# The opening of a fused convolution and gated-MLP kernel: first columns of w_in by another queue, two taps to TensorE, scaling and loads in another order

## The chip, the cores and the metric

The kernel runs on one core of a Trainium2 chip. The metric is device time in microseconds (us) of a whole execution. The engines are TensorE (PE; its weight loads are shown as PEld), VectorE (DVE), ScalarE (ACT), GpSimd (POOL) and SyncE (SP). Each executes its own instructions in order. DMAs are issued by SP, ACT or POOL, each in a queue of its own, and carried by 16 DMA engines that the queues share. A DMA that changes the type (fp32 to bf16) is issued by POOL here; the others by SP or ACT.

## The reference

The input x has 8 batches of 4096 tokens with 192 channels. A causal convolution of 7 taps runs over the tokens, its weights being a softmax over the taps for each of 8 heads of 24 channels. The result goes through a gated layer without a gate matrix of its own:

```python
w = np.exp(weight - np.max(weight, axis=-1, keepdims=True))
w = w / (np.sum(w, axis=-1, keepdims=True) + 1e-09)          # (8 heads, 7 taps)
out = np.einsum('hk,bskhg->bshg', w, x_unf)                  # x_unf: 7 shifted copies of x
h = out.reshape(32768, 192) @ w_in                           # w_in (192, 2048)
g = h * (1.0 / (1.0 + np.exp(-beta * h)))                    # beta (2048,)
y = g @ w_out                                                # w_out (2048, 192)
```

The kernel computes silu(beta * h) and multiplies w_out by 1/beta, which gives the same. x, w_in, w_out and beta are fp32 in memory; the large matrix products are done in bf16.

## The kernel before, in words

**Stages and units.** The tokens are cut into 32 chunks; a chunk is 512 tokens of two batches at once. Channels lie on partitions: a group is 64 channels (rows 0 to 63 for one batch, 64 to 127 for the other), and there are NG = 3 groups. One chunk is one stage `s`, and a stage has 16 units `u`, one for each block of 128 columns of w_in. `hidden` (L409) does six matmuls of a unit into a PSUM tile ph, and one ScalarE activation (L417) writes g from it. `output` (L442) does matmuls of g with w_out in pairs, into two PSUM tiles pa and pb, spread over the units behind. From stage 1 on a unit has 8 pairs; in stage 0 units 3 and 7 have 5 pairs into pa alone and units 8 to 15 have 5 each; what is left over is done after the last stage. Finished sums go through VectorE (L460) and an SP DMA.

**Convolution.** For chunks from 2 on, x is cast, transposed by DMA and convolved on VectorE tap by tap (`tap`, L331 and L333), a stage ahead, out of a `queue` of seven taps. In stage 0 the order of such work is written out by hand in `first_work`: for each unit a list, in which `None` takes the next tap from the queue.

**The opening.** Chunks 0 and 1 are done differently, and all of this stands ahead of the units or in stage 0:
- SP issues x of chunk 0 (x0, two DMAs), x of chunk 1 (x1, two), the first two quarters of w_out (w_out_raw), x of chunk 2 (xf, two), the other two quarters, x of chunk 3. ACT issues weight and beta.
- POOL builds a selection matrix `sel` and an identity, then issues w_in, as bf16, into w_in_s: columns 0 to 255 for each half of the partitions (two DMAs, L208), then, after a tiny copy `hold` that waits for the first cast of x0, columns 256 to 511 and the three other quarters of 512 columns, two DMAs each.
- The softmax: VectorE takes the maximum on 8 partitions, ScalarE the exponentials and their sum, and a matmul with `sel` spreads them to 128 partitions (L254), where VectorE divides, which gives cw. beta is transposed by TensorE (L258) and copied by ScalarE (L259).
- `fill` (L226) gives TensorE matmuls of zeros where it would be idle.
- x0 is cast (VectorE, L231), transposed by TensorE (L238) and copied to xt0 by ScalarE (L299). VectorE builds `diag`, seven diagonal matrices of cw (L302). Groups 0 and 1 of chunk 0 are convolved by TensorE, seven matmuls with `diag` each (L284), and copied out to ct by ScalarE (L326); group 2 is convolved by VectorE in seven taps, which end in ct too. In between ScalarE casts x1 to x1b (L231), two blocks after each group's matmuls.
- VectorE scales the first quarter of w_out by 1/beta (`scale_w_out`, L311). The other three quarters are scaled by it from `first_work`.
- Unit 0 of stage 0 does the hidden matmuls of units 0 and 1 group by group, then `second` transposes x1b on TensorE (L353) and copies it out on VectorE (L362). Group 0 of chunk 1 is convolved by TensorE in units 4 to 6 (`CONV1`) and copied out by VectorE (`conv1_evac`, L388); its groups 1 and 2 are the seven taps of the queue. `rows_of(2)` casts chunk 2 and starts its transposes.

Of the kernel before, what the change touches and what calls it, by code (L numbers as in the profile page):

```python
# [9 lines left out]
FP32 = mybir.dt.float32  # L10
FP32R = mybir.dt.float32r
BF16 = mybir.dt.bfloat16
AF = mybir.ActivationFunctionType
ALU = mybir.AluOpType
# [3 lines left out]
def kernel(  # L18
# [17 lines left out]
    nc = tc.nc  # L36

    B, S, D = x.shape
    H, K = weight.shape
    F = moe_w_in.shape[1]  # L40
    group = D // H
    DG = 64
    NG = D // DG
    HP = group // NG
    TOK = 512
    NF = F // 128
    PAD = K - 1
    HALO = 16
# [7 lines left out]
    NB = TOK // BLK  # L56
# [4 lines left out]
    consts = ctx.enter_context(tc.tile_pool(name="consts", bufs=1))  # L61
    setup = ctx.enter_context(tc.tile_pool(name="setup", bufs=1))
# [18 lines left out]
    def in_a():  # L81
        return psum_a.tile([128, 2, TOK], FP32, name="pa")
# [50 lines left out]
    NW = 4  # L133
    FW = F // NW
# [11 lines left out]
    def load_w_out(i):  # L146
        fcs = slice(i * NQ, (i + 1) * NQ)
        nc.sync.dma_start(out=w_out_raw[:, fcs, :], in_=w_out_v[:, fcs, :])

    e8 = setup.tile([H, K + 1], FP32)  # L150
    cw8 = setup.tile([H, K], FP32)
    beta_q = setup.tile([NF, 128], FP32)
    nc.scalar.dma_start(out=cw8, in_=weight)
    nc.scalar.dma_start(out=beta_q, in_=moe_beta.rearrange("(c p) -> c p", p=128))


    def load_x(dst, t0):
        for i in range(2):
            t = t0 + i * 2 * BLK
            nc.sync.dma_start(  # L160
                out=dst[:, i].rearrange("q h b d -> q h (b d)"),
                in_=x_v[0, t : t + 2 * BLK, :, :].rearrange(
                    "(q b) h d -> q h (b d)", b=2
                ),
            )

    load_x(x0, 0)
    load_x(x1, TOK)
    load_w_out(0)
    load_w_out(1)  # L170
    load(2)
    load_w_out(2)
    load_w_out(3)
    load(3)

    zeros = setup.tile([128, TOK], BF16)
    nc.vector.memset(zeros, 0.0)
    warm = setup.tile([H, 1], FP32)
    nc.vector.memset(warm, 0.0)  # L179
    nc.scalar.activation(warm, warm, AF.Exp)  # L180

    sel = setup.tile([H, 2, DG], FP32)
    nc.gpsimd.memset(sel, 1.0)
# [22 lines left out]
    def load_w_in(c0, c1):  # L206
        for r in range(2):
            nc.gpsimd.dma_start(  # L208
                out=w_in_s[r * DG : (r + 1) * DG, :, c0:c1], in_=w_in_v[:, :, c0:c1]
            )  # L210

    load_w_in(0, FW // 2)

    nmax = setup.tile([H, 1], FP32)
    nc.vector.reduce_max(nmax, cw8, axis=mybir.AxisListType.X, negate=True)
    nc.scalar.activation(
        e8[:, 0:K], cw8, AF.Exp, bias=nmax, accum_out=e8[:, K : K + 1]
    )
    nc.scalar.activation(warm, warm, AF.Silu)
    ident_b = setup.tile([128, 128], BF16)  # L220
    nc.vector.tensor_copy(ident_b, ident)
    pf = psum_h.tile([128, 2, TOK], FP32, name="ph")

    def fill(n, cols=TOK):
        for _ in range(n):
            nc.tensor.matmul(  # L226
                pf[:, 0, 0:cols], zeros[:, 0:128], zeros[:, 0:cols], start=True, stop=True
            )

    def cast_rows(copy, xb, x, b):  # L230
        copy(  # L231
            xb[:, b].rearrange("q c h p -> q h c p"),
            x[:, b // 2, :, b % 2].rearrange("q h (p c) -> q h c p", c=NG),
        )
# [7 lines left out]
    def tokens(xt, b):  # L242
        t = HALO + (b // 2) * 2 * BLK
        return xt[:, :, t : t + 2 * BLK].rearrange("p c (q b) -> p c b q", b=2)[:, :, b % 2]

    beta = consts.tile([128, NF], FP32)
    beta_r = setup.tile([128, NF], FP32)
    cw = consts.tile([128, K], FP32)
    rn = setup.tile([128, 1], FP32)

    fill(5)
    pc = in_a()
    pw, pb = pc[:, 0, 0 : K + 1], pc[:, 1, 0:NF]
    nc.tensor.matmul(  # L254
        pw, sel.rearrange("i h p -> i (h p)"), e8, start=True, stop=True
    )
    fill(1, 256)
    nc.tensor.transpose(pb, beta_q, ident[0:NF, 0:NF])  # L258
    nc.scalar.copy(beta, pb)  # L259
    for b in range(2):  # L260
        cast_rows(nc.vector.tensor_copy, x0b, x0, b)
    nc.vector.reciprocal(rn, pw[:, K : K + 1])
    nc.vector.tensor_scalar_mul(cw, pw[:, 0:K], rn)
    for b in range(2, NB):
        cast_rows(nc.vector.tensor_copy, x0b, x0, b)

    hold = setup.tile([1, 1], BF16)
    nc.gpsimd.tensor_copy(hold, x0b[0:1, 0, 0, 0, 0:1])  # L268
    load_w_in(FW // 2, FW)
    for i in range(1, NW):  # L270
        load_w_in(i * FW, (i + 1) * FW)

    diag = setup.tile([128, K, 128], FP32R)
    xt0 = setup.tile([128, NG, HALO + TOK], FP32R)
    nc.vector.memset(xt0[:, :, 0:HALO].bitcast(FP32), 0.0)
    xt1 = setup.tile([128, HALO + TOK], FP32R)
    cts = {}

    def new_ct(s):
        cts[s] = ct_pool.tile([128, NG, TOK], BF16, name="ct")  # L280

    def diag_tap(k, xt, pv, rows=slice(0, 128)):
        o = HALO - PAD + k
        nc.tensor.matmul(  # L284
            pv,
            diag[rows, k, :],
            xt[rows, o : o + TOK],
            start=(k == 0),
            stop=(k == K - 1),
        )  # L290

# [4 lines left out]
    for b in range(NB):  # L296
        pt = pts[b % 2][:, b // 2, 0 : NG * BLK].rearrange("p (c q) -> p c q", c=NG)
        transposes(pt, x0b, b)
        nc.scalar.copy(tokens(xt0, b), pt)  # L299
        fill(1, 256 if b % 2 else 128)  # L300
    fill(1, 256)
    nc.vector.tensor_tensor(  # L302
        diag,
        ident.unsqueeze(1).to_broadcast((128, K, 128)),
        cw.unsqueeze(2).to_broadcast((128, K, 128)),
        ALU.mult,
    )

    def scale_w_out(i):
        fcs = slice(i * NQ, (i + 1) * NQ)  # L310
        nc.vector.tensor_tensor(  # L311
            w_out_s[:, fcs, :],
            w_out_raw[:, fcs, :],
            beta_r[:, fcs].unsqueeze(2).to_broadcast((128, NQ, D)),
            ALU.mult,
        )
# [3 lines left out]
    for c in range(NG - 1):  # L320
        pv = in_b() if c else psum_h.tile([128, 2, TOK], FP32, name="ph")
        for k in range(K):
            diag_tap(k, xt0[:, c], pv[:, 0, :])
        for b in range(2):
            cast_rows(nc.scalar.copy, x1b, x1, 2 * c + b)
        nc.scalar.copy(cts[0][:, c, :], pv[:, 0, :])  # L326

    def tap(dst, src, k):
        scalar = cw[:, k : k + 1]
        if k == 0:  # L330
            nc.vector.tensor_scalar_mul(dst, src, scalar)  # L331
        else:
            nc.vector.scalar_tensor_tensor(  # L333
                out=dst, in0=src, scalar=scalar, in1=dst, op0=ALU.mult, op1=ALU.add
            )

    for k in range(K):
        o = HALO - PAD + k
        tap(cts[0][:, NG - 1, :], xt0[:, NG - 1, o : o + TOK].bitcast(FP32), k)
    nc.vector.reciprocal(beta_r, beta)  # L340
    scale_w_out(0)

# [164 lines left out]
    def rows_of(ch):  # L507
        for h in range(2):
            cast(ch, h)
        xpose(ch)  # L510


    first_work = {
        4: [None],
        5: [lambda: scale_w_out(1), None],
        7: [None, conv1_evac],
        8: [None],
        9: [lambda: scale_w_out(2)],
        10: [None, lambda: rows_of(2)],
        11: [None],  # L520
        12: [lambda: scale_w_out(3), None],
    }

    queue = deque()
    for s in range(N_ST):
        jobs_of(s)
        for u in range(NF):
            if s > 0 or u > 1:
                hidden(s, u)
            elif u == 0:  # L530
                phs = [hidden(0, fc, [0]) for fc in range(2)]
                for j in range(1, NG):
                    for fc in range(2):
                        hidden(0, fc, [j], phs[fc])
                second()
            if s > 0:
                output(s, u, 8 if s < N_ST - 1 else 7, "ab")
            elif u > 7:
                output(s, u, 5, "ab")
            elif u == 3 or u == 7:  # L540
                output(s, u, 5, "a")
            if s == 0:
                if u in CONV1:
                    conv1(u)
                if u == min(CONV1):
                    queue.extend(conv_ops(1, 1))
                for work in first_work.get(u, []):
                    (work or queue.popleft())()
            else:
                if u % 2 and queue:  # L550
                    queue.popleft()()

                if u == 0 and s + 3 < N_CH:
                    load(s + 3)
                if u < 2 and s + 2 < N_CH:
                    cast(s + 2, u)
                if u == 1 and s + 2 < N_CH:
                    xpose(s + 2)
            if u == 12 and s + 2 < N_CH:
                queue.extend(conv_ops(s + 2, 0))  # L560
# [32 lines left out]
```

## Time and profile before

| what | value |
|---|---|
| median of 10 runs | 692.58 us (692.06 to 693.34) |
| profiled execution | 692.36 us |
| its span, first to last instruction | 690.6 us |
| busy: PE, ACT, DVE, POOL | 683.7, 579.1, 527.1, 8.1 us |
| chain that ended last | PE 96%, DMA 2%, DVE 1% |
| first g of stage 0 (L417) starts | 13.63 us |
| first hidden matmuls of stage 1 start | 31.43 us |

The times are counted from the span's start. The chain is followed back from the last instruction, at each step to what released it. In rows of the timeline the columns are start, duration, engine, line, operation, what is written and read with its shape, the count of merged instructions, and in brackets the idle time of the engine ahead of it with what ended it. Ends of matmuls are modelled. DMA queue q1 is SP's, q10 ACT's, q0 POOL's.

### The profile page before, as it was taken

To read this page: it belongs to the slowest core of one execution; us is meant where nothing else is said; L and a number is where in the kernel's file an instruction comes from. 1 tells how busy PE (TensorE), PEld (TensorE's weight loads), DVE (VectorE), ACT (ScalarE), POOL (GpSimd) and SP (SyncE) were. 2 spreads that over 40 slices of the span, in tenths; PEclk is the share of its full clock that TensorE was granted. 3 is DMA by queue.
4 is the path that set the end of the run, shared out by engine and by line. 5 is a ranking of instruction groups with operands and counts; after the bars stand their busy time and mean duration, and the time that the engine had idled before them with its cause. 6 is when DMAs were issued, how large, how long until landed. Compare 5 with 4: busy or idle time off the path is not lost.

```text
span 690.6 us, 24335 instructions
## 1 busy us (share of the span) xinstructions
PE 683.7 (99%) x11310; PEld 496.5 (72%) x11310; DVE 527.1 (76%) x466; ACT 579.1 (84%) x531; POOL 8.1 (1%) x20
## 2 busy tenths in 40 slices
PE   8999999999999999999999999999999999999997
PEld 4677777777777777777777777777777777777776
DVE  7888877797777797777887777887777977777712
ACT  7888888888888888888888888888888888888893
POOL 4000000000000000000000000000000000000000
PEclk9999999999999999999999999999999999999999
DMA  9754332344332343332344432443323433322111
GB/s 219 170 117 116 93 104 70 83 116 113 91 104 59 100 116 104 97 98 60 108 116 94 104 83 70 116 116 93 104 62 92 116 107 97 104 54 60 48 37 59
DMA packets 121862, 66.86 MB, mean 97 GB/s; under 512 B 53265, under 2 KB 121761, under 8 KB 121761
## 3 DMA queue, kind: packets, MB, share of 16 engines
q1 hardware_dynamic: 119632, 63.73, 35.0%
q0 software_dynamic: 2080, 1.57, 1.5%
q8 instruction: 88, 1.44, 0.9%
q14 instruction: 14, 0.11, 0.1%
q10 hardware_dynamic: 48, 0.01, 0.0%
HBM read 29.89 MB, written 25.17 MB: 80 GB/s over the span
## 4 chain that ended last, share of the span: by engine, by line
PE 96%; DMA 2%; DVE 1%; POOL 0%; ACT 0%; issue 0%
PE ph L409 47%; PE pa L442 24%; PE pb L442 24%; DMA w_in_s<-in_moe_w_in_dram 2%; DVE ct L333 1%; DMA x<-in_x_dram 0%; PE pb L284 0%; POOL w_in_s L208 0%; DVE w_out_s L311 0%; DVE ct L388 0%; DVE xb L106 0%; ACT g L417 0%; DVE x0b L231 0%; ACT osb L458 0%; POOL hold L268 0%
## 5 line engine op out<-in xcount | busy, mean ns | idle before, releaser
L417 ACT ACTIVATE g<-ph,beta 128x1024 bf16<-128x1024 f32 x512 | 569.8, 1114 | 97.1 <-PE ph L409 91.2
L442 PEld LDWEIGHTS <-g 64*128 64x128 bf16 x8160 | 353.6, 94 | 120.9 <-ACT g L417 0.9
L409 PE MATMUL ph<-ct,w_in_s 64*128 64x512 bf16 x3072 | 417.0, 376 | 1.6 <-ACT g L417 0.7
L333 DVE SCALAR_TENSOR_TENSOR ct<-xt,cw,ct 128x1536 bf16<-128x1536 bf16 (+2 forms) x192 | 338.4, 1762 | 2.5
L442 PE MATMUL pa<-w_out_s,g 64*128 64x192 bf16 x4112 | 238.9, 243 | 0.6 <-ACT g L417 0.5
L442 PE MATMUL pb<-w_out_s,g 64*128 64x192 bf16 (+1 forms) x4048 | 224.9, 243 | 0.0
L409 PEld LDWEIGHTS <-w_in_s 64*128 64x128 bf16 x3072 | 142.8, 94 | 64.0 <-DMA w_in_s<-in_moe_w_in_dram 2.2
L460 DVE TENSOR_REDUCE osb<-pa 128x384 f32<-128x768 f32 x64 | 61.3, 958 | 121.5 <-PE pa L442 121.5
L460 DVE TENSOR_REDUCE osb<-pb 128x384 f32<-128x768 f32 x63 | 60.3, 958 | 28.9 <-PE pb L442 28.8
L106 DVE CAST xb<-xf 128x768 bf16<-128x768 f32 x60 | 40.7, 679 | 0.0
L331 DVE TENSOR_SCALAR ct<-xt,cw 128x1536 bf16<-128x1536 bf16 (+2 forms) x32 | 31.2, 974 | 0.2 <-ACT xt L299 0.2
L208 POOL DMA_DIRECT2D w_in_s<-in_moe_w_in_dram x10 | 6.5, 656 | 2.3 <-DMA w_in_s<-in_moe_w_in_dram 2.3
L458 ACT COPY osb<-pb 128x192 f32<-128x192 f32 x1 | 0.3, 319 | 6.7 <-PE pb L442 6.7
L226 PE MATMUL ph<-zeros 128*128 128x512 bf16 (+2 forms) x11 | 4.4, 493 | 1.3 <-DVE warm L179 1.3
L284 PE MATMUL pb<-xt,diag 64*128 64x512 f32 (+1 forms) x21 | 5.1, 445 | 0.0
L121 DVE COPY xt<-xt 128x18 bf16<-128x18 bf16 x27 | 4.3, 161 | 0.0
L311 DVE TENSOR_TENSOR w_out_s<-w_out_raw,beta_r 128x768 bf16<-128x768 f32 x4 | 3.8, 959 | 0.0
L284 PEld LDWEIGHTS pb<-xt,diag 64*128 64x128 f32 (+1 forms) x21 | 3.2, 187 | 0.8
L284 PE MATMUL ph<-xt,diag 128*128 128x512 f32 x7 | 2.8, 562 | 0.2 <-ACT xt L299 0.2
L226 PEld LDWEIGHTS <-zeros 128*128 128x128 bf16 x11 | 1.4, 139 | 2.1 <-DVE warm L179 1.3
L231 DVE CAST x0b<-x 128x384 bf16<-128x384 f32 x4 | 1.5, 408 | 1.8 <-DMA x<-in_x_dram 1.8
L180 ACT ACT_TABLE_LOAD x1 | 1.3, 1283 | 1.8 <-issue 1.8
(48 smaller groups left out, 25.0 us busy)
## 6 DMA issues: line engine op xcount, KB each, us to landing
out_dram<-osb SPq DMA_DIRECT2D x127, 192.0 KB, 2.1
xf<-in_x_dram SPq DMA_DIRECT2D x60, 384.0 KB, 4.2
xt<-xb SPq DMA_TRANSPOSE x120, 3.0
x<-in_x_dram SPq DMA_DIRECT2D x4, 384.0 KB, 4.5
w_out_raw<-in_moe_w_out_dram SPq DMA_DIRECT2D x4, 384.0 KB, 13.3
w_in_s<-in_moe_w_in_dram POOLq DMA_DIRECT2D x6, 192.0 KB, 11.7
w_in_s<-in_moe_w_in_dram POOLq DMA_DIRECT2D x4, 96.0 KB, 8.7
out_dram<-osb SPq DMA_DIRECT2D x2, 96.0 KB, 1.6
```

The lines of the kernel that those rows point to most:

```text
L106: nc.vector.tensor_copy(xbs[ch][:, :, :, h, :], xfs[ch][:, h].rearrange("q b (p c) -> q b c p", c=NG),)
L121: nc.vector.tensor_copy(dst, last[:, :, HALO + TOK - PAD :])
L208: nc.gpsimd.dma_start(out=w_in_s[r * DG : (r + 1) * DG, :, c0:c1], in_=w_in_v[:, :, c0:c1])
L226: nc.tensor.matmul(pf[:, 0, 0:cols], zeros[:, 0:128], zeros[:, 0:cols], start=True, stop=True)
L284: nc.tensor.matmul(pv, diag[rows, k, :], xt[rows, o : o + TOK], start=(k == 0), stop=(k == K - 1),)
L311: nc.vector.tensor_tensor(w_out_s[:, fcs, :], w_out_raw[:, fcs, :], beta_r[:, fcs].unsqueeze(2).to_broadcast((128, NQ, D)), ALU.mult,)
L331: nc.vector.tensor_scalar_mul(dst, src, scalar)
L333: nc.vector.scalar_tensor_tensor(out=dst, in0=src, scalar=scalar, in1=dst, op0=ALU.mult, op1=ALU.add)
L409: nc.tensor.matmul(ph[:, h, :], w_in_s[rows, j, fc * 128 : (fc + 1) * 128], cts[s][rows, j, :], start=(j == 0), stop=(j == NG - 1),)
L417: nc.scalar.activation(gs[s][:, fc], ph, AF.Silu, scale=beta[:, fc : fc + 1])
L442: nc.tensor.matmul(self.po[:, r, b * D : (b + 1) * D], g[rows, fc, self.h, q * BLK : (q + 1) * BLK], w_out_s[rows, fc, :], start=(self.don ...
L460: nc.vector.tensor_reduce(dst, self.po[:, :, 0 : nb * D].rearrange("p r n -> p n r"), axis=mybir.AxisListType.X, op=ALU.add,)
```

## The change

- **w_in.** Columns 0 to 255 are no longer loaded by POOL. SP loads them as fp32 into a new tile w_in_raw, for both halves of the partitions in one DMA whose source is broadcast over a leading dimension of 2, and ScalarE copies them to w_in_s as bf16. This copy stands after beta's copy and ahead of the casts of x1. POOL issues columns 256 to 511 and the three other quarters, all after `hold`: 8 DMAs instead of 10.
- **Loads on SP.** x0, then beta (from ACT's queue before), then w_in_raw, x1, three quarters of w_out, x of chunk 2, the last quarter, x of chunk 3.
- **Softmax.** The raw taps are spread to 128 partitions by the matmul first; maximum, exponentials, sum and division are then done there. `diag` is built in three pieces, the first between the casts of x0.
- **Group 2 of chunk 0.** Taps 5 and 6 are done by TensorE in two matmuls, taps 0 to 4 by VectorE, which then adds the two.
- **Scaling of w_out's first quarter** is done by GpSimd.
- **Order.** The tile of zeros has 128 columns and is broadcast; the fills have other numbers and places; xt0's halo is cleared earlier; beta's transpose comes after those of x0; the last cast of x1 stands after the copies to ct.
- **Stage 0.** `first_work` is rewritten: the scaling of quarters 1, 2 and 3 is in units 4, 6 and 8 (5, 9 and 12 before), conv1_evac and rows_of(2) in unit 6 (7 and 10), the seven taps in units 4, 4, 5, 6, 8, 9, 10 (4, 5, 7, 8, 10, 11, 12). Units 4 and 7 have 2 and 5 output pairs into pa, unit 15 has 10: 52 pairs in all instead of 50. `CONV1` is as before.

```diff
-    e8 = setup.tile([H, K + 1], FP32)
-    cw8 = setup.tile([H, K], FP32)
+    w8 = setup.tile([H, K], FP32)
+    nc.scalar.dma_start(out=w8, in_=weight)
     beta_q = setup.tile([NF, 128], FP32)
-    nc.scalar.dma_start(out=cw8, in_=weight)
-    nc.scalar.dma_start(out=beta_q, in_=moe_beta.rearrange("(c p) -> c p", p=128))
...
     load_x(x0, 0)
+    nc.sync.dma_start(out=beta_q, in_=moe_beta.rearrange("(c p) -> c p", p=128))
+    F0 = 256
+    w_in_raw = setup.tile([128, NG, F0], FP32)
+    nc.sync.dma_start(
+        out=w_in_raw, in_=w_in_v[:, :, 0:F0].unsqueeze(0).to_broadcast((2, DG, NG, F0))
+    )
     load_x(x1, TOK)
-    load_w_out(0)
-    load_w_out(1)
+    for i in range(NW - 1):
+        load_w_out(i)
     load(2)
-    load_w_out(2)
-    load_w_out(3)
+    load_w_out(NW - 1)
     load(3)
...
-    load_w_in(0, FW // 2)
-
-    nmax = setup.tile([H, 1], FP32)
-    nc.vector.reduce_max(nmax, cw8, axis=mybir.AxisListType.X, negate=True)
-    nc.scalar.activation(
-        e8[:, 0:K], cw8, AF.Exp, bias=nmax, accum_out=e8[:, K : K + 1]
-    )
...
+    fill(3)
+    pw = in_a()[:, 0, 0:K]
+    nc.tensor.matmul(pw, sel.rearrange("i h p -> i (h p)"), w8, start=True, stop=True)
+    fill(5)
...
+    nc.vector.reduce_max(nmax, pw, axis=mybir.AxisListType.X, negate=True)
+    nc.scalar.activation(cw, pw, AF.Exp, bias=nmax, accum_out=total)
+    nc.scalar.activation(warm, warm, AF.Silu)
+    nc.vector.reciprocal(total, total)
+    nc.vector.tensor_scalar_mul(cw, cw, total)
...
-    for b in range(2):
+    for b in range(NB):
         cast_rows(nc.vector.tensor_copy, x0b, x0, b)
...
+        if b == 1:
+            diags(0, 2)
+    diags(2, 4)
+    diags(4, K)
...
     nc.gpsimd.tensor_copy(hold, x0b[0:1, 0, 0, 0, 0:1])
-    load_w_in(FW // 2, FW)
+    load_w_in(F0, FW)
     for i in range(1, NW):
         load_w_in(i * FW, (i + 1) * FW)
...
         nc.scalar.copy(tokens(xt0, b), pt)
-        fill(1, 256 if b % 2 else 128)
+        if b % 2:
+            fill(1, 384)
+    pb = in_a()[:, 0, 0:NF]
+    nc.tensor.transpose(pb, beta_q, ident[0:NF, 0:NF])
+    nc.scalar.copy(beta, pb)
     fill(1, 256)
...
+    nc.scalar.copy(w_in_s[:, :, 0:F0], w_in_raw)
...
-        nc.vector.tensor_tensor(
+        (nc.vector if i else nc.gpsimd).tensor_tensor(
             w_out_s[:, fcs, :],
...
-        for b in range(2):
-            cast_rows(nc.scalar.copy, x1b, x1, 2 * c + b)
+        for b in ((0, 1), (2,))[c]:
+            cast_rows(nc.scalar.copy, x1b, x1, b)
         nc.scalar.copy(cts[0][:, c, :], pv[:, 0, :])
+    cast_rows(nc.scalar.copy, x1b, x1, NB - 1)
...
-    for k in range(K):
+    K_V = 5
+    pv = in_a()[:, 0, :]
+    for k in range(K_V, K):
+        diag_tap(k, xt0[:, NG - 1], pv, k0=K_V)
+    dst = cts[0][:, NG - 1, :]
+    for k in range(K_V):
         o = HALO - PAD + k
-        tap(cts[0][:, NG - 1, :], xt0[:, NG - 1, o : o + TOK].bitcast(FP32), k)
+        tap(dst, xt0[:, NG - 1, o : o + TOK].bitcast(FP32), k)
+    nc.vector.tensor_tensor(dst, pv, dst, ALU.add)
...
     first_work = {
-        4: [None],
-        5: [lambda: scale_w_out(1), None],
-        7: [None, conv1_evac],
-        8: [None],
-        9: [lambda: scale_w_out(2)],
-        10: [None, lambda: rows_of(2)],
-        11: [None],
-        12: [lambda: scale_w_out(3), None],
+        4: [None, lambda: scale_w_out(1), None],
+        5: [None],
+        6: [conv1_evac, lambda: scale_w_out(2), lambda: rows_of(2), None],
+        8: [None, lambda: scale_w_out(3)],
+        9: [None],
+        10: [None],
     }
 
+    QUOTA_A = {4: 2, 7: 5}
...
-                output(s, u, 5, "ab")
-            elif u == 3 or u == 7:
-                output(s, u, 5, "a")
+                output(s, u, 5 if u < NF - 1 else 10, "ab")
+            elif u in QUOTA_A:
+                output(s, u, QUOTA_A[u], "a")
```

`diags(k0, k1)` is a new function around the multiplication of L302, for the taps k0 to k1.

More of the change, by code (lines that the diff above doesn't have):

```diff
@@ L167 @@
     load_x(x0, 0)
+    nc.sync.dma_start(out=beta_q, in_=moe_beta.rearrange("(c p) -> c p", p=128))
[4 more added lines that the diff above has]
+    )
     load_x(x1, TOK)
-    load_w_out(0)
-    load_w_out(1)
+    for i in range(NW - 1):
+        load_w_out(i)
     load(2)
-    load_w_out(2)
-    load_w_out(3)
+    load_w_out(NW - 1)
     load(3)
-    zeros = setup.tile([128, TOK], BF16)
+    zeros = setup.tile([128, 128], BF16)
     nc.vector.memset(zeros, 0.0)
@@ L180 @@
     nc.scalar.activation(warm, warm, AF.Exp)
+    xt0 = setup.tile([128, NG, HALO + TOK], FP32R)
+    nc.vector.memset(xt0[:, :, 0:HALO].bitcast(FP32), 0.0)
     sel = setup.tile([H, 2, DG], FP32)
@@ L210, in load_w_in @@
             )
-    load_w_in(0, FW // 2)
-    nmax = setup.tile([H, 1], FP32)
-    nc.vector.reduce_max(nmax, cw8, axis=mybir.AxisListType.X, negate=True)
-    nc.scalar.activation(
-        e8[:, 0:K], cw8, AF.Exp, bias=nmax, accum_out=e8[:, K : K + 1]
-    )
-    nc.scalar.activation(warm, warm, AF.Silu)
     ident_b = setup.tile([128, 128], BF16)
@@ L224, in fill @@
     def fill(n, cols=TOK):
+        zc = zeros.unsqueeze(1).to_broadcast((128, cols // 128, 128))
         for _ in range(n):
-            nc.tensor.matmul(
-                pf[:, 0, 0:cols], zeros[:, 0:128], zeros[:, 0:cols], start=True, stop=True
-            )
+            nc.tensor.matmul(pf[:, 0, 0:cols], zeros, zc, start=True, stop=True)
     def cast_rows(copy, xb, x, b):
@@ L244, in tokens, with diags @@
         return xt[:, :, t : t + 2 * BLK].rearrange("p c (q b) -> p c b q", b=2)[:, :, b % 2]
+    fill(3)
+    pw = in_a()[:, 0, 0:K]
+    nc.tensor.matmul(pw, sel.rearrange("i h p -> i (h p)"), w8, start=True, stop=True)
+    fill(5)
+    nmax = setup.tile([128, 1], FP32)
+    total = setup.tile([128, 1], FP32)
+    cw = consts.tile([128, K], FP32)
+    nc.vector.reduce_max(nmax, pw, axis=mybir.AxisListType.X, negate=True)
[3 more added lines that the diff above has]
+    nc.vector.tensor_scalar_mul(cw, cw, total)
     beta = consts.tile([128, NF], FP32)
     beta_r = setup.tile([128, NF], FP32)
[L248 to L259, printed above, removed]
-    for b in range(2):
+    diag = setup.tile([128, K, 128], FP32R)
+    def diags(k0, k1):
+        nc.vector.tensor_tensor(
+            diag[:, k0:k1],
+            ident.unsqueeze(1).to_broadcast((128, k1 - k0, 128)),
+            cw[:, k0:k1].unsqueeze(2).to_broadcast((128, k1 - k0, 128)),
+            ALU.mult,
+        )
+    for b in range(NB):
         cast_rows(nc.vector.tensor_copy, x0b, x0, b)
[L262 to L265, printed above, removed]
+        if b == 1:
+            diags(0, 2)
+    diags(2, 4)
+    diags(4, K)
     hold = setup.tile([1, 1], BF16)
     nc.gpsimd.tensor_copy(hold, x0b[0:1, 0, 0, 0, 0:1])
-    load_w_in(FW // 2, FW)
+    load_w_in(F0, FW)
     for i in range(1, NW):
         load_w_in(i * FW, (i + 1) * FW)
-    diag = setup.tile([128, K, 128], FP32R)
-    xt0 = setup.tile([128, NG, HALO + TOK], FP32R)
-    nc.vector.memset(xt0[:, :, 0:HALO].bitcast(FP32), 0.0)
     xt1 = setup.tile([128, HALO + TOK], FP32R)
@@ L280, in new_ct, with diag_tap @@
         cts[s] = ct_pool.tile([128, NG, TOK], BF16, name="ct")
-    def diag_tap(k, xt, pv, rows=slice(0, 128)):
+    def diag_tap(k, xt, pv, rows=slice(0, 128), k0=0):
         o = HALO - PAD + k
@@ L287, in diag_tap @@
             xt[rows, o : o + TOK],
-            start=(k == 0),
+            start=(k == k0),
             stop=(k == K - 1),
@@ L299 @@
         nc.scalar.copy(tokens(xt0, b), pt)
-        fill(1, 256 if b % 2 else 128)
-    fill(1, 256)
-    nc.vector.tensor_tensor(
[L303 to L307, printed above, removed]
+        if b % 2:
[3 more added lines that the diff above has]
+    nc.scalar.copy(beta, pb)
+    fill(1, 256)
+    nc.scalar.copy(w_in_s[:, :, 0:F0], w_in_raw)
     def scale_w_out(i):
         fcs = slice(i * NQ, (i + 1) * NQ)
-        nc.vector.tensor_tensor(
+        (nc.vector if i else nc.gpsimd).tensor_tensor(
             w_out_s[:, fcs, :],
```

## The prediction

> **What bounds the kernel now.** I read the page first: TensorE is busy for 683.7 of 690.6 us and the chain of work that ended last is 96% TensorE. From 33 us on the units follow each other without a gap, six hidden matmuls and sixteen output matmuls each. Such a stretch has no slack: a delay of the opening moves the end by its own length, and a saving there does the same. The change touches only the first of the 32 stages, so what counts is one moment: when the first hidden matmuls of stage 1 start. In the timeline of TensorE that is 31.43 us (the row below, with its sixteen output matmuls behind it).
>
> ```profile
> 31.43 0.83 PE L409 MATMUL ph<-ct,w_in_s 64*128 64x512 bf16 x6
> 32.07 0.67 PE L442 MATMUL pa<-w_out_s,g 64*128 64x192 bf16 x8
> 32.58 0.49 PE L442 MATMUL pb<-w_out_s,g 64*128 64x192 bf16 x8
> ```
>
> Then the chain of the first 36 us: it waits for x, then for w_in, which the POOL queue brings, then runs over conv1 and VectorE's taps.
>
> ```profile
> 0.81 3.42 DMA x<-in_x_dram
> 5.05 1.96 POOL w_in_s L208 x3
> 7.00 10.94 DMA w_in_s<-in_moe_w_in_dram
> 23.22 1.28 DVE ct L333
> ```
>
> Then the timeline of ScalarE, which executes in order and which the change gives a new instruction:
>
> ```profile
> 6.96 0.50 ACT L299 CAST xt<-ph 128x384 fp32r<-128x384 bf16 x1
> 7.35 1.33 ACT L231 CAST x1b<-x 128x384 bf16<-128x384 f32 x2
> 10.35 0.59 ACT L326 CAST ct<-ph 128x512 bf16<-128x512 f32 x1 [1.67 <-PE ph L284]
> 10.83 1.34 ACT L231 CAST x1b<-x 128x384 bf16<-128x384 f32 x2
> 12.05 0.61 ACT L326 CAST ct<-pb 128x512 bf16<-128x512 f32 x1
> 13.63 4.31 ACT L417 ACTIVATE g<-ph,beta 128x1024 bf16<-128x1024 f32 x4 [0.97 <-PE ph L409]
> 18.85 1.12 ACT L417 ACTIVATE g<-ph,beta 128x1024 bf16<-128x1024 f32 x1 [0.91 <-PE ph L409]
> ```
>
> The first g stands at 13.63. Sixteen of them at 1.067 us (the steady 8.54 us for 8) would take 17.1 us; they end at 32.3, so 1.6 us are lost on the way, mostly to w_in landing late.
>
> Last, the DMA view in three windows (3 to 5, 14 to 20 and 22 to 26 us; columns are packets, MB, share of 16 engines):
>
> ```profile
> q1 hardware_dynamic: 499, 0.72, 104.2%
> q0 software_dynamic: 830, 0.78, 76.9%
> q1 hardware_dynamic: 832, 0.62, 41.0%
> q1 hardware_dynamic: 1656, 1.23, 102.9%
> ```
>
> Per engine that is a packet of 1536 B (x) each 64 ns (2 us x 16 / 499), a packet of 768 B (w_out, xf) each 38.6 ns (4 x 16 / 1656), and where SP's and POOL's queues both have work, one of each in 115 ns (6 x 16 / 832). So a POOL packet of w_in (2 KB read, 1 KB written) costs about 77 ns. A packet of 1 KB from SP lies between: about 47 ns.
>
> **What the Trainium skill says.** (1) "DMA: Bandwidth & Descriptors", section "Rules for kernel authors": the number of engines follows from the slowest dimension of both access patterns, and "a leading zero-stride broadcast of c copies" confines the whole DMA to at most c engines. The section "Why a DMA increments its semaphore by 16 and not by 1" adds that SP's transfers then take the lowest-numbered engines. The trace of before agrees as far as it can: the load of weight (8 rows) left 8 data packets and 8 of 4 B, beta (16 rows) 16 and 16, the 48 packets of q10; every large load has 128 rows or 64. No broadcast is in it. (2) The same page, "Queues, rings and completion order": on each engine, descriptors are consumed in ring order. The landings agree: SP's transfers of before land in issue order, x at 4.24, 5.27, 6.90 and 10.59, w_out at 12.58 and 15.03. (3) "TensorE: Matmul & The Clock Gate", Part 1: after an idle window TensorE runs at half rate for some 3.4 us of work. The trace: the first seven diagonal taps take 2.80 us, the next seven 1.79. (4) "GPSIMD Engine Reference", section "Performance versus the Vector engine": 2.6 cycles per element for a two-input elementwise operation, so 768 elements are an estimated 1.7 us; the trace has none.
>
> **The change part by part.**
>
> *The first 256 columns of w_in* leave the POOL queue (2 DMAs of 96 KB there) and come as fp32 on SP, behind x0 and beta, ahead of x1: one DMA with 2 x 192 rows of 1 KB, whose source begins with a broadcast dimension of 2. By (1) it runs on two engines, 192 packets on each. The two engines are free of x0 at 5.2 us. The 192 packets take 192 x 47 ns = 9.0 us. POOL's queue meanwhile has 8 DMAs of 192 packets, 96 on each engine: 24 small ones (some 48 ns, half-size) and 72 of 77 ns, 1.2 + 5.5 = 6.7 us. Both queues take turns, and at least 96 of the 192 are still to go when POOL's packets start (at the latest about 4.1 us after the first issue at 5.0, since in the packet records of before q0's first, issued at 2.17, moved at 6.3; by 9.1 us some 83 are done). So all POOL packets fall inside: 5.2 + 9.0 + 6.7 = 20.9, landed at about **21.0 us**.
>
> *What is queued behind it.* On these two engines x1 stands behind in ring order: 16 packets of 64 ns for each half, landed at about 22.0 and 23.0 instead of 6.90 and 10.59. Then w_out 0 to 2 at 32 x 38.6 ns = 1.24 us each: 24.2, 25.4, 26.7; x of chunk 2 by 29, w_out 3 at 30.4. SP itself is held too (it took 3 us to issue one xf[...] in before), but nothing lands later for that: the two rings stay full.
>
> *The copy of w_in on ScalarE* (w_in_raw to w_in_s, 128x768) stands after the beta copy, ahead of the x1b casts and the ct copies. Its cost is about 0.85 us, between the 0.59 of 512 columns and 1.07 of 1024. Its wait is the matter: ScalarE reaches it at 7.7 and starts at 21.0. Queued behind: x1b 0 and 1 (1.33, from 22.0 to 23.3), ct 0 (0.59, 23.9), x1b 2 (24.6), ct 1 (25.2), x1b 3 (25.9). TensorE's hidden matmuls wait for ct; it has done its 16 diagonal taps by 12.5 and is cold. After ct 1 three pairs of matmuls must pass before g can start: 0.92 us in before (12.71 to 13.63), about 1.5 cold. The first g starts at 26.7, that is 13.1 us later than 13.63.
>
> *From the first g to stage 1.* In before 17.8 us (13.63 to 31.43). All of w_in has landed by then, so the 1.6 us of losses are gone; cold TensorE costs about 0.9 in the transposes of x1 and the third unit. 17.1 us: stage 1 starts at 43.8, **12.4 us late**. VectorE's own chain fits under this: its work from the x1 transposes on took 13.96 to 31.10 with 1.6 idle, so from 27.6 it ends at about 43.2.
>
> *Two taps of the third group to TensorE.* VectorE drops two of 0.78 us and gains one addition out of PSUM (about 0.6), TensorE gains two matmuls of 0.26 to 0.40. Worth up to 1 us where nothing waits; here hidden under the wait for w_in (VectorE done at 13, needed at 25.2). If that cover is gone, see the first rival.
>
> *Scaling of w_out quarter 0 to GpSimd*: 0.96 us leaves VectorE, 1.7 (estimate) appear on POOL once w_out 0 is in, 24.2 to 25.9; its first reader is the fifth unit, at about 31. Nothing, bounds 0 and +0.5.
>
> *Softmax after the spread, diagonals in three pieces, fewer DMAs on ACT's queue, the fills*: all end before 8 us, with 13 us to spare. Nothing here; with the wait gone they are worth -0.5 to +0.5.
>
> *w_out quarter 3 of 4 ahead of chunk 2, scaling and casts moved in the units, pairs*: every landing is before its reader. Stage 0 does 52 pairs instead of 50: two pairs, four matmuls at 41 ns (0.66 for 16), 0.16 us less at the end.
>
> Sum: +13.1 - 1.6 + 0.9 - 0.16 = **+12.2 us**. The profiled execution took 692.36 (span 690.6 and 1.8 around it), so 704.6; the median is 0.2 above it: **704.8 us**.
>
> **Rivals.** *A, sixteen engines after all* (the instruction carries the rows in another order): not slower. Then w_in_raw lands at about 7.0 (one x transfer of 1.7 us after x0), the copy is free, and the first g stands at 12.8 to 13.4, set by TensorE's 16 taps and the addition. The losses of 1.6 go. Together 0.9 to 2.2 us gained, less what VectorE waits for w_out: about 690.9. The point from which it decides: at 16 engines each has 24 packets, 1.1 us; the wait starts to cost once fewer than about 8 share the load (48 packets, 2.3 us, still near 8). For it speaks only that the trace of before shows no confined transfer; against it the skill's sentence, which names this very shape.
> *B, two engines, but POOL's packets do not hold it up* (served late, or SP first): landed at 5.2 + 9.0 = 14.3, stage 1 about 5.5 us late: 698.0. Against it the equal counts of 830 and 832 packets.
> *C, two engines and each packet dearer*, at the 64 ns of the larger x packets: 12.3 us instead of 9.0, 708.1.
>
> **How the numbers follow.** The main case has 0.72 (its own range 701 to 707), B 0.10, C 0.07, A 0.11. A measurement of this kernel tells about 0.2% (1.4 us) from no change. A divides into 0.06 faster, 0.04 same, 0.01 slower; the others are slower. The range 697.5 to 708.5 takes in most of B and half of C and leaves out A.
>
> **What would show it.** w_in_raw's landing 15 us or more after its issue; on ScalarE a wait of some 13 us before a copy of 128x768 to w_in_s; first g near 26.7, stage 1 near 43.8; the DMA share low between 8 and 20 us; TensorE idle from 12.5 to 24. I am wrong if w_in_raw lands by 9 us.

## The result, and the profile after

The changed kernel takes 705.58 us in the median (704.62 to 706.04, 8 runs), the kernel before 692.63 (691.54 to 693.34, 29 runs). The ratio is 1.0187, with a 95% interval of 1.0178 to 1.0196: 12.95 us slower, where 12.2 were forecast. The profiled execution took 705.34, its span is 703.6.

The loads of x as SP issues them in the kernel before, and then the timeline of SP's queue in the changed kernel (start, duration of the issue):

```profile
0.81 2.00 SPq L160 DMA_DIRECT2D x<-in_x_dram  x4
```

```profile
2.34 0.70 SPq L169 DMA_DIRECT2D w_in_raw<-in_moe_w_in_dram  x1
3.09 7.00 SPq L158 DMA_DIRECT2D x<-in_x_dram  x2
10.13 10.60 SPq L148 DMA_DIRECT2D w_out_raw<-in_moe_w_out_dram  x3
```

The broadcast load itself is issued in 0.70 us. The two loads of x1 behind it took 1.0 us to issue in the kernel before and take 7.00 here; the three quarters of w_out take 10.60.

From the timeline of ScalarE, where the first g stood at 13.63 before:

```profile
7.48 0.19 ACT L311 COPY beta<-pa 128x16 f32<-128x16 f32 x1
20.37 0.83 ACT L313 CAST w_in_s<-w_in_raw 128x768 bf16<-128x768 f32 x1 [12.69 <-DMA w_in_raw<-in_moe_w_in_dram]
22.94 1.29 ACT L228 CAST x1b<-x 128x384 bf16<-128x384 f32 x2 [1.74 <-DMA x<-in_x_dram]
24.14 0.58 ACT L332 CAST ct<-ph 128x512 bf16<-128x512 f32 x1
24.61 0.70 ACT L228 CAST x1b<-x 128x384 bf16<-128x384 f32 x1
25.21 0.59 ACT L332 CAST ct<-pb 128x512 bf16<-128x512 f32 x1
25.69 0.72 ACT L228 CAST x1b<-x 128x384 bf16<-128x384 f32 x1
27.42 2.12 ACT L430 ACTIVATE g<-ph,beta 128x1024 bf16<-128x1024 f32 x2 [1.01 <-PE ph L422]
```

Two waits follow each other: 12.69 us for w_in_raw, and then 1.74 for x1, which had landed at 6.90 in the kernel before. The copies to ct, which TensorE waits for, stand behind both in ScalarE's order. The first g is 13.79 us late.

Rows of TensorE in the same stretch, and where stage 1 begins:

```profile
11.04 0.63 PE L291 MATMUL pa<-xt,diag 128*128 128x512 f32 x2
24.76 2.98 PE L422 MATMUL ph<-ct,w_in_s 64*128 64x512 bf16 x12 [13.10 <-ACT ct L332]
45.02 0.83 PE L422 MATMUL ph<-ct,w_in_s 64*128 64x512 bf16 x6
```

It has done the sixteen diagonal taps by 11.7 and then idles for 13.10 us. The first twelve hidden matmuls take 2.98 us, at half rate: the granted clock from 24.7 to 27.8 us was 0.50. Stage 1 begins at 45.02 instead of 31.43.

In the chain of the first 48 us x1 is the last of these waits, not w_in_raw; two of its rows:

```profile
3.09 19.82 DMA x<-in_x_dram
22.94 1.29 ACT x1b L228 x2
```

From there little is regained. Laid beside each other, the first g of each stage is late by 13.79 us in stage 0, by 13.59 in stage 1 and by 13.43 in stage 2; in stage 31 it is 13.43 still. After the last g the changed kernel needs 11.76 us where the other needed 12.22. So the span is 13.0 us longer.

That two engines carry the load is seen in the trace's records of semaphore additions and of packets. The first half of x0, which uses all sixteen engines, adds to its semaphore sixteen times as data lands, from 3.64 to 4.21. The load of weight, which has 8 rows, shows one early addition, at 1.50, and eight as data lands, from 2.08 to 2.17. The load of w_in_raw shows one early addition, at 3.43, and then two alone, at 20.32 and 20.34. In the four kernels below that have this form of load there are exactly two late ones as well. What stands behind it is split the same way: the first half of x1 has fourteen additions by 16.70, themselves later than in the kernel before, and the last two at 22.88 and 22.91.

The packets agree. Those of w_in_raw are 384 of 1 KB, with a median of 46 ns each; two engines could take 43 of them in a microsecond. Between 5 and 6 us 44 start. From 13 to 20 us it is only 15 or 16 in each microsecond, with POOL's packets in between. In the first experiment below, with the same bytes as two DMAs, up to 194 start in one microsecond.

### The profile page after: what moved, and what is told of

It reads as the page before. It is cut to its first block, busy times and chain, and to the rows that moved or that the text cites. A ratio compares the mean times of both kernels' runs of the same rounds, so it can differ in the third digit from the quotient of the medians.

```text
span 703.6 us, 24339 instructions
## 1 busy us (share of the span) xinstructions
PE 685.6 (97%) x11312; PEld 521.4 (74%) x11312; DVE 523.1 (74%) x466; ACT 579.9 (82%) x532; POOL 8.4 (1%) x19
## 3 DMA queue, kind: packets, MB, share of 16 engines
q0 software_dynamic: 1664, 1.38, 1.4%
## 4 chain that ended last, share of the span: by engine, by line
PE 95%; DMA 3%; ACT 1%; SPq 0%; issue 0%; ACTq 0%
PE ph L422 47%; PE pa L455 24%; PE pb L455 24%; DMA x<-in_x_dram 3%; ACT g L430 0%; ACT x1b L228 0%; PE pb L291 0%; ACT ct L332 0%; SPq L158 0%; SPq L169 0%; SPq L166 0%; ACT osb L471 0%; ACTq L430 0%
## 5 line engine op out<-in xcount | busy, mean ns | idle before, releaser
L455 PEld LDWEIGHTS <-g 64*128 64x128 bf16 x8160 | 369.7, 94 | 103.9 <-ACT g L430 0.7
L422 PE MATMUL ph<-ct,w_in_s 64*128 64x512 bf16 x3072 | 425.9, 378 | 13.5 <-ACT ct L332 13.1
L455 PE MATMUL pa<-w_out_s,g 64*128 64x192 bf16 x4112 | 245.3, 243 | 0.5 <-ACT g L430 0.5
L455 PE MATMUL pb<-w_out_s,g 64*128 64x192 bf16 (+1 forms) x4048 | 230.3, 243 | 0.0
L422 PEld LDWEIGHTS <-w_in_s 64*128 64x128 bf16 x3072 | 159.4, 94 | 69.2 <-ACT w_in_s L313 10.0
L228 ACT CAST x1b<-x 128x384 bf16<-128x384 f32 x4 | 2.7, 702 | 1.7 <-DMA x<-in_x_dram 1.7
## 6 DMA issues: line engine op xcount, KB each, us to landing
w_out_raw<-in_moe_w_out_dram SPq DMA_DIRECT2D x4, 384.0 KB, 14.9
```

Source lines behind the costliest of these rows:

```text
L422: nc.tensor.matmul(ph[:, h, :], w_in_s[rows, j, fc * 128 : (fc + 1) * 128], cts[s][rows, j, :], start=(j == 0), stop=(j == NG - 1),)
L455: nc.tensor.matmul(self.po[:, r, b * D : (b + 1) * D], g[rows, fc, self.h, q * BLK : (q + 1) * BLK], w_out_s[rows, fc, :], start=(self.don ...
```

## Experiments

The theory is that of the prediction: the broadcast dimension of 2, being outermost, confines the load to two engines, and what stands behind it on these engines, and on ScalarE, waits. Rivals are that the load's size and place do it, that other parts of the change cost too, that POOL's packets have no share in it, and that only the copy's own wait matters. The first four ran on one chip beside the kernel before (692.58 us in the median of 33 runs), the other four on another (692.40 of 33). Three of the eight were measured in a single execution each. In the profiles of all versions, these three too, the time from the first g of stage 1 to that of stage 31 is 627.7 or 627.8 us, so what sets them apart lies ahead of that stretch or behind it.

**The same load as two DMAs.** The broadcast is replaced by one DMA for each half of the partitions, in the same place:

```diff
-    nc.sync.dma_start(
-        out=w_in_raw, in_=w_in_v[:, :, 0:F0].unsqueeze(0).to_broadcast((2, DG, NG, F0))
-    )
+    for r in range(2):
+        nc.sync.dma_start(out=w_in_raw[r * DG : (r + 1) * DG], in_=w_in_v[:, :, 0:F0])
```

> The changed kernel, with the first columns of w_in loaded by two DMAs on SP (64 rows of partitions each, the same 393 KB in the same place of the queue) instead of one DMA with a broadcast leading dimension. Theory (two engines carry the broadcast load, and x1, w_out and ScalarE's copy wait behind it): w_in_raw lands at about 7 us instead of 20.3, the first g stands at 12.8 to 13.4, the time is 690.4 to 692.0 us. Rival (the broadcast form is harmless, the wait comes from the load's size and place in SP's queue, or from the copy's place on ScalarE): w_in_raw lands near 20 us still and the time stays at 704 to 706.

Measured: 691.25 us (690.99 to 692.08, 21 runs), ratio to the kernel before 0.9983, interval 0.9977 to 0.9990. ScalarE:

```profile
8.18 0.83 ACT L314 CAST w_in_s<-w_in_raw 128x768 bf16<-128x768 f32 x1 [0.63 <-DMA w_in_raw<-in_moe_w_in_dram]
9.33 1.32 ACT L229 CAST x1b<-x 128x384 bf16<-128x384 f32 x2 [0.32 <-DMA x<-in_x_dram]
13.19 4.15 ACT L431 ACTIVATE g<-ph,beta 128x1024 bf16<-128x1024 f32 x4 [0.36 <-PE ph L423]
```

The waits of 12.69 and 1.74 us are 0.63 and 0.32, and the same bytes in the same place of the queue landed at 6.88 and 8.10. It is the form of the load that costs 14.3 us (705.58 against 691.25), and the rival of size and place falls. This version is also faster than both kernels, by 1.3 us against the one before.

**The w_in part alone**, in the kernel before:

```diff
     load_x(x0, 0)
+    F0 = 256
+    w_in_raw = setup.tile([128, NG, F0], FP32)
+    nc.sync.dma_start(
+        out=w_in_raw, in_=w_in_v[:, :, 0:F0].unsqueeze(0).to_broadcast((2, DG, NG, F0))
+    )
     load_x(x1, TOK)
...
-    load_w_in(0, FW // 2)
...
     fill(1, 256)
+    nc.scalar.copy(w_in_s[:, :, 0:F0], w_in_raw)
```

> The kernel before with the w_in part alone: the broadcast load on SP behind x0, POOL's first two DMAs left out, the copy on ScalarE behind the copies to xt0. Theory: all of the loss comes with this part, the load lands at 20 to 21 us, time 704 to 707. Rival (the other parts, such as the new order in stage 0 or GpSimd's scaling, cost several us of the 13): 692 to 700.

Measured: 706.51 us (4 runs), ratio 1.0206 (1.0190 to 1.0222). All of the loss is here. It is 0.9 us more than that of the changed kernel, but the two intervals overlap (from 1.0190 here, to 1.0196 there), so this alone does not show that the other parts give something back. Its ScalarE line:

```profile
20.91 0.83 ACT L305 CAST w_in_s<-w_in_raw 128x768 bf16<-128x768 f32 x1 [13.37 <-DMA w_in_raw<-in_moe_w_in_dram]
```

**The rest alone**, that is, the changed kernel with columns 0 to 255 loaded by POOL again:

```diff
-    w_in_raw = setup.tile([128, NG, F0], FP32)
-    nc.sync.dma_start(
-        out=w_in_raw, in_=w_in_v[:, :, 0:F0].unsqueeze(0).to_broadcast((2, DG, NG, F0))
-    )
...
+    load_w_in(0, F0)
     ident_b = setup.tile([128, 128], BF16)
...
-    nc.scalar.copy(w_in_s[:, :, 0:F0], w_in_raw)
```

> The changed kernel without its w_in part: POOL loads columns 0 to 255 as in the kernel before, no copy on ScalarE, everything else changed. Theory: the rest is worth -1.0 to +0.5 us where nothing waits, so 691.6 to 693.1. Rival (the rest costs too): 694 or more.

Measured: 691.72 us (691.09 to 692.49, 13 runs), ratio 0.9990 (0.9982 to 0.9998): 0.9 us gained. The profiled execution was the slowest of the 13 (692.49) and no faster than the kernel before, with a span of 690.7; it shows where its gain went in stage 0. The first g stands at 13.36, 0.27 us earlier than before, but that of stage 1 at 32.86, 0.57 later. VectorE waits for transfers that come later than it now wants them, and TensorE then waits for VectorE:

```profile
17.18 0.96 DVE L314 TENSOR_TENSOR w_out_s<-w_out_raw,beta_r 128x768 bf16<-128x768 f32 x1 [0.61 <-DMA w_out_raw<-in_moe_w_out_dram]
24.30 0.69 DVE L106 CAST xb<-xf 128x768 bf16<-128x768 f32 x1 [1.31 <-DMA xf<-in_x_dram]
25.50 0.68 DVE L106 CAST xb<-xf 128x768 bf16<-128x768 f32 x1 [0.52 <-DMA xf<-in_x_dram]
29.70 0.34 PE L452 MATMUL pa<-w_out_s,g 64*128 64x192 bf16 x4 [1.05 <-DVE w_out_s L314]
```

In the version with two DMAs x of chunk 2 landed at 22.59 and 23.87, here at 24.27 and 25.48. How much of this a faster execution loses was not looked at. w_in's first columns on SP are worth another 0.5 us (691.72 to 691.25; the means differ by 0.49, with a 95% interval of 0.2 to 0.8), if their load uses all engines.

**POOL's loads after the broadcast load has landed.** The tiny copy that holds POOL's queue reads w_in_raw:

```diff
-    nc.gpsimd.tensor_copy(hold, x0b[0:1, 0, 0, 0, 0:1])
+    nc.gpsimd.tensor_copy(hold, w_in_raw[0:1, 0, 0:1])
```

> The changed kernel, broadcast load kept, but POOL's eight DMAs are issued only when w_in_raw has landed (hold reads it instead of x0b). This measures the two-engine load with its engines to itself. Theory: without POOL's packets in between it lands at 14 to 15.5 us (192 packets of 47 to 52 ns per engine from 5.2 on) instead of 20.3, the time is 698 to 702 since w_in follows late. Rival (SP's packets go first in any case, and the load is slow for another reason): it lands at 19 to 21 as before.

Measured in one execution: 700.38 us. ScalarE:

```profile
14.77 0.83 ACT L313 CAST w_in_s<-w_in_raw 128x768 bf16<-128x768 f32 x1 [7.18 <-DMA w_in_raw<-in_moe_w_in_dram]
20.12 2.12 ACT L430 ACTIVATE g<-ph,beta 128x1024 bf16<-128x1024 f32 x2 [1.01 <-PE ph L422]
24.38 1.11 ACT L430 ACTIVATE g<-ph,beta 128x1024 bf16<-128x1024 f32 x1 [2.15 <-PE ph L422]
```

Alone on its engines the load landed at 14.74. x0's last part had landed at 5.29, so 192 packets took 9.45 us, 49 ns each. The further 5.6 us to 20.34 are POOL's packets, taken in between. The 2.15 us before the third g belong to this version alone: w_in itself, now issued from 14.9 on, is late, and TensorE waits 0.96 and 0.24 us for it.

**A load that nobody reads.** The kernel before with the broadcast load on SP and nothing else; all of w_in still comes by POOL:

```diff
     load_x(x0, 0)
+    F0 = 256
+    w_in_raw = setup.tile([128, NG, F0], FP32)
+    nc.sync.dma_start(
+        out=w_in_raw, in_=w_in_v[:, :, 0:F0].unsqueeze(0).to_broadcast((2, DG, NG, F0))
+    )
     load_x(x1, TOK)
```

> The kernel before, with nothing changed but one more load: the broadcast load of w_in_raw on SP between x0 and x1, whose result nobody reads (POOL still loads all of w_in, ScalarE has no copy). Theory: on its two engines x1 and w_out stand behind the load in ring order, so x1's first half lands at 23 to 24.5 us instead of 6.9, the casts of x1 on ScalarE wait for it, and the time is 705 to 708 though the load itself is waited for by no one. Rival (only ScalarE's wait for w_in_raw costs): x1 lands by 9 and the time is 692 to 694.

Measured in one execution: 707.69 us, 15 us slower than the kernel before. ScalarE:

```profile
7.17 0.50 ACT L304 CAST xt<-ph 128x384 fp32r<-128x384 bf16 x1
24.48 1.29 ACT L236 CAST x1b<-x 128x384 bf16<-128x384 f32 x2 [16.81 <-DMA x<-in_x_dram]
29.57 2.12 ACT L422 ACTIVATE g<-ph,beta 128x1024 bf16<-128x1024 f32 x2 [1.61 <-PE ph L414]
```

No instruction waits for w_in_raw, and the harm is larger than in the changed kernel: w_in_raw landed at 23.58, behind the ten DMAs of POOL instead of eight, and the first half of x1 at 24.45 (fourteen of its engines were done by 19.49). The place ahead of x1 is enough. In the changed kernel x1 comes last too, so moving ScalarE's copy alone should not help there; that was not tried.

**The broadcast load in ACT's queue:**

```diff
     nc.scalar.dma_start(out=w8, in_=weight)
+    F0 = 256
+    w_in_raw = setup.tile([128, NG, F0], FP32)
+    nc.scalar.dma_start(
+        out=w_in_raw, in_=w_in_v[:, :, 0:F0].unsqueeze(0).to_broadcast((2, DG, NG, F0))
+    )
...
-    F0 = 256
-    w_in_raw = setup.tile([128, NG, F0], FP32)
-    nc.sync.dma_start(
-        out=w_in_raw, in_=w_in_v[:, :, 0:F0].unsqueeze(0).to_broadcast((2, DG, NG, F0))
-    )
```

> The changed kernel with the broadcast load issued in ACT's queue instead of SP's. Theory: x1 no longer stands behind it in a ring and lands by 12 us, but the two engines are now shared by three queues, so w_in_raw itself lands at 22 to 27 us and ScalarE's copy, which stands ahead of the casts of x1, waits as long: 705 to 711. Rival (the harm lies in SP's ring alone, another queue mends it): w_in_raw lands by 12 and the time is 690 to 694.

Measured in one execution: 710.84 us, the slowest of all.

```profile
27.54 0.83 ACT L313 CAST w_in_s<-w_in_raw 128x768 bf16<-128x768 f32 x1 [19.48 <-DMA w_in_raw<-in_moe_w_in_dram]
28.27 1.29 ACT L228 CAST x1b<-x 128x384 bf16<-128x384 f32 x2
```

x1 no longer stands behind the load: it landed at 10.53 and 12.96. But the load now shares its two engines with SP's packets as well as POOL's and lands at 27.51. SP's first quarter of w_out shows it too: fourteen engines had brought their part by 11.50, the last two at 16.59 and 17.41. Another queue is not another set of engines.

**x1 ahead of w_in_raw**, with the two-DMA form and ScalarE's copy behind the first copy to ct; the edit is shown against the version with two DMAs, which was measured once more beside it:

```diff
     load_x(x0, 0)
...
+    load_x(x1, TOK)
     for r in range(2):
         nc.sync.dma_start(out=w_in_raw[r * DG : (r + 1) * DG], in_=w_in_v[:, :, 0:F0])
-    load_x(x1, TOK)
...
-    nc.scalar.copy(w_in_s[:, :, 0:F0], w_in_raw)
...
         nc.scalar.copy(cts[0][:, c, :], pv[:, 0, :])
+        if c == 0:
+            nc.scalar.copy(w_in_s[:, :, 0:F0], w_in_raw)
```

> The changed kernel with w_in_raw loaded by two DMAs, placed behind x1 on SP, and ScalarE's copy of it behind the first copy to ct. Theory: the two waits of ScalarE in the version with x1 behind (0.63 and 0.32 us) go, the first g moves from 13.19 to 12.7 to 13.0, limited by TensorE's sixteen taps and VectorE's addition: 690.7 to 691.3. Rival (w_in_raw, now later, is waited for itself): 691.3 to 692.

> The changed kernel with w_in_raw loaded by two DMAs ahead of x1, once more beside the version with x1 ahead: 690.9 to 691.7 again, and 0 to 0.5 us above the other.

Measured: 692.05 us (691.63 to 692.92, 13 runs) with x1 first, ratio 0.9994 (0.9986 to 1.0003), and 691.35 (690.82 to 692.22, 21 runs) with w_in_raw first, ratio 0.9987 (0.9980 to 0.9993). With w_in_raw first the time is the expected one, but 0.7 us below the other and not 0 to 0.5 above. The theory's number for x1 first (up to 691.3) was wrong. The rival (up to 692) has the reason right and is 0.05 short:

```profile
9.01 0.59 ACT L332 CAST ct<-ph 128x512 bf16<-128x512 f32 x1
10.98 0.83 ACT L334 CAST w_in_s<-w_in_raw 128x768 bf16<-128x768 f32 x1 [1.38 <-DMA w_in_raw<-in_moe_w_in_dram]
13.87 5.17 ACT L432 ACTIVATE g<-ph,beta 128x1024 bf16<-128x1024 f32 x5 [0.36 <-PE ph L424]
```

w_in_raw landed at 10.89. ScalarE waits 0.53 us for x1 and 1.38 for w_in_raw; with w_in_raw first it was 0.32 for x1 and 0.63 for w_in_raw in the earlier profile, and 0.86 for x1 alone in the one beside this. The first g is 0.7 to 0.8 us later than with w_in_raw first (13.87 against 13.19 and 13.11). The order of the changed kernel was the better one.

## Why the prediction was right

- **Two engines.** Right. The sentence in the Trainium skill, page "DMA: Bandwidth & Descriptors", section "Rules for kernel authors", that a leading zero-stride broadcast of c copies confines a DMA to at most c engines, agrees with this case: two late semaphore additions, and 20.34 us against 8.10 for the same bytes as two DMAs.
- **The load's time.** 21.0 forecast, 20.34 measured. Its terms: 9.0 us for the packets alone, 9.45 measured from the landing of x0; 6.7 for POOL's, 5.6 measured. The step that all of POOL's 96 packets on an engine fall inside was wrong. POOL's eight DMAs landed at 11.87, 13.09, 14.74, 16.41, 18.06, 19.75, 21.37 and 23.37, so when the load was done two of them were still to finish. What it saved there, x1 paid.
- **x1 behind it.** 22.0 and 23.0 forecast, 22.91 and 24.04 measured, because of POOL's remaining packets. With this the chain's last wait is x1's, by more than forecast.
- **ScalarE's sequence and the first g.** 26.7 forecast, 27.42 measured: 0.9 us late from x1, and 0.2 regained, since the first g follows the first cast of x1 after 4.48 us where 4.7 were forecast. The order of the operations was as worked out, and the copy took 0.83 against 0.85.
- **From the first g to stage 1.** 17.1 us forecast, 17.60 measured (27.42 to 45.02). The 1.6 us of lost time were to go and 0.9 to be lost to cold matmuls. From the first g to that of stage 1 it was 18.66 us before and 18.46 after, so only 0.2 was regained. The cold start shows in a gap of 0.55 us before the third g; the ten output pairs of the last unit, which I had not priced there, hold stage 1's first hidden matmuls for some 0.4 us more than five would.
- **The end.** 0.16 us less forecast, 0.46 measured (12.22 to 11.76 after the last g); 0.25 of it is TensorE's own stretch, the rest lies behind it. Another 0.16 came back in stage 1 (13.59 late to 13.43). Stage 1 was 1.2 us later than forecast (45.02 against 43.8), and these two made good about half of it: that the sum is off by only 0.8 us (13.0 against 12.2) is in part luck.
- **The parts said to be hidden.** Right: they cost nothing, and with the cover gone the rest alone gained 0.9 us; the prediction had up to 1 us for the two taps and -0.5 to +0.5 for the softmax and the fills. How the 0.9 divides among them was not measured. Two terms: the first seven diagonal taps take 1.86 us where they took 2.80, since TensorE is at full rate nearly from their start (they follow each other every 0.23 us after the first, where before it was 0.43 or more until 9.4 us); the scaling on GpSimd takes 1.47 against an estimate of 1.7 from the Trainium skill, page "GPSIMD Engine Reference", section "Performance versus the Vector engine".
- **The rivals.** A, sixteen engines, was not this kernel, but its 690.9 fits the version with two DMAs (691.25), though w_in_raw landed at 8.10 there and not at 7.0. B gave the landing of the load without POOL's share, 14.3, which measured 14.74. C's 64 ns for a packet were 49.
- **The signs.** The landing 18.0 us after the issue, ScalarE's wait of 12.69 us and TensorE's idle time from 11.7 to 24.8 came as named. One sign did not: the DMA share between 8 and 20 us was not low, 1.09 of the sixteen engines' time against 1.19 in the kernel before. It was low only from 5 to 8 us (0.45 against 0.95); after that the other fourteen engines had POOL's loads, x1 and w_out.

Left open: POOL's first DMA was done on fourteen engines by 9.67 us and on the last two only at 11.75 and 11.87. In the first microseconds these two engines took fewer of POOL's packets than one for each of SP's; the runs do not show why.

## What to carry to other kernels

Look at the outermost dimension of every load: here a broadcast of two copies in the source turned a transfer of some 2.5 us (5.57 to 8.10 as two DMAs) into one of 9.45 with its engines to itself and of 15 beside other traffic. What was issued later in that queue stood behind it on the same engines, whether or not anyone read the result. Other numbers of copies were not tried. Write such a load as one DMA for each copy. Before a load is placed early in a queue, list what stands behind it in that queue and in the engine that waits for it; here ScalarE waited 12.69 us for the load and 1.74 more for x1 behind it, and in the experiments either wait alone cost at least as much as both (707.69 us with no reader, 710.84 with x1 not behind the load).

## What the runs showed of the hardware that was not expected

- A confined load with no reader cost 15.3 us in one execution (707.69 against 692.40). That lies in the range expected for it, but it is more than the same load with a reader and less work on POOL's queue (705.58 against 692.63).
- Moving the load to ACT's queue freed x1 (10.53 instead of 22.91) and made the load itself 7.2 us later (27.51 instead of 20.34), just past the 22 to 27 expected.
- Two queues on one engine did not share it evenly from the start, as told above; later, from 13 us on, POOL's DMAs followed each other on these engines every 1.6 to 2.0 us.
